# Two weight pairs instead of four beside attention, with conversion spread over more steps

## The chip, the cores and the metric

The kernel runs on one core of a Trainium2 chip. A core has TensorE (PE in the profile, with its weight loads as PEld), VectorE (DVE), ScalarE (ACT), GpSimd (POOL) and SyncE (SP, which here only issues DMAs). The metric is the time of one execution on the device in microseconds; less is better.

## The reference

Three layers follow one another on 2304 tokens of 512 features.

```python
# 1. block-causal attention: 4 batches, 8 heads, 576 tokens, 64 features a head
scores = q @ k.T / 8;  mask: key block (64 tokens) not later than the query's block
attn = softmax(scores);  x = attn @ v          # x: [2304, 512]
# 2. squared ReLU, d_ff = 2048
h = x @ w_in;  g = s * relu(h)**2 + b;  x = g @ w_out
# 3. top-1 of 8 experts, each [512, 1024] and [1024, 512]
e = argmax(x @ w_gate + bias[modality]);  out = gate[e] * (relu(x @ w1[e]) @ w2[e])
```

`moe_w_in` and `moe_w_out` reach the kernel as float64, and float32 precision is kept by splitting each operand into a high and a low part, so that each product is three matmuls (`PASSES`: high-high, high-low, low-high).

## The kernel before

**Attention** (`attention`, lines 25 to 254) is a generator. It works on 16 units, each two heads of one batch (a batch has four units), and each unit has nine steps, one for each block of 64 queries: 144 steps, and some more in which the last ones drain. Step t issues the scores of its block (matmuls L137 and L140, the row maximum L142 on DVE, the exponential L147 on ACT), the normalising of the step before (reciprocal L159 on DVE, product L160 on POOL), the transposes of the block of five steps before (L179, copied by L185), and P·V seven steps after the scores (L202, copied by L204). The ninth step of a unit has two row maxima, the others one. When a unit is done, its 128 features of x go to DRAM (`xT_d`, L207), from which the next layer reads them.

**The squared-ReLU layer** (`SquaredRelu`) takes tokens in 9 blocks of 256 and d_ff in 8 pairs of 256 columns. `load_x` reads a block's x (L311), and makes its high part on ACT (L314) and its low part on DVE (L315). `hidden` does one pair on one block: 24 matmuls (L377), ReLU on ACT (L381), square on DVE (L382), high and low part of the result (L385, L386). `project` multiplies by that pair's rows of `w_out`: 6 matmuls for each half of the block (L392).

Blocks 0 to 5 can begin beside attention, since their tokens lie in batches that are done before the last (`begun` is 6). Blocks 6 to 8 hold tokens of the last batch. `NA` says how many pairs each of the first six blocks does beside attention: 2 for block 0 and 4 for the others, 22 pair-blocks in all. `_beside` cuts this work into pieces: for each block one piece for x, one for each pair, and two for the projections, whose sums go to DRAM (`part_d`, L417). `plan` lists the block of each piece, `NA + 3` for each block, 40 pieces. The main loop emits piece n after step `PIECE_0 + n * PIECE_D`, if its weights and its tokens are ready; the pieces that are left come after the loop:

```python
            while (emitted < len(plan) and step >= PIECE_0 + emitted * PIECE_D
                   and converted >= 4 * NA[plan[emitted]] + 3 and done >= ...):
                next(pieces)
                emitted += 1
        for _ in pieces:
            pass
```

**Conversion.** A pair's weights are four chunks. `convert` handles one chunk in three turns: the DMA of 512 KB (L320); the float64 bits made float32 by three instructions on DVE (L329 to L331); the high part on ACT (L364) and then the low part on POOL (L335). `CONV` lists the steps in which a turn is taken: 19 turns for 16 chunks, at steps 8, 12, ... 80. A turn's instructions stand behind the attention instructions issued last on their engines.

**The next stage** (`after`, L419) does what is left, in groups of one block and a range of pairs: first pairs 0 to 4 of the late blocks 6, 7 and 8; then pairs `NA[blk]` to 4 of the begun blocks (before: block 0 alone, pairs 2 and 3); then pairs 4 to 8 of all blocks in the order 6, 7, 8, 0, ... 5. Beside this the other four pairs are converted (`load_w`, all on DVE and ACT), one chunk for each unit (a unit here is one pair on one block). A group's x is loaded during the group before it; there are two buffers for it. Sums of earlier pairs are read back from `part_d` (L601), added to the new ones (`collect`, L609, or copied where there are none, L611), and written again or, at the end, passed to the router. The layers after this are untouched by the change.

The order of each engine's instructions is fixed before the run by a planner, which takes them by the order of emission and lets later ones go ahead only where they are ready by its own estimate.

Of the kernel before, what the change touches and what calls it, by code (L numbers as in the profile page):

```python
# [278 lines left out]
class SquaredRelu:  # L279
# [115 lines left out]
    def beside(self, ctx, blocks):  # L395

        self.pools(ctx, "a", 1, 2, max(NA), "raw cv xr x r g")
        rows = ctx.enter_context(self.tc.tile_pool(name="ma_rows", bufs=1))
        return self._beside(blocks, rows)

    def _beside(self, blocks, rows):
        nc, D = self.nc, self.D
        for blk in blocks:
            x = self.load_x(blk)
            yield blk
            g = []
            n = NA[blk]
            for p in range(n):
# [11 lines left out]
    def after(self, ctx, rt, begun, free, routed):  # L420

        nc = self.nc
        wz = ctx.enter_context(self.tc.tile_pool(name="m_wz", bufs=1, reuse_waits="tile"))
        self.pools(ctx, "b", 2, 2, 3, "r g xr raw cv x")
        wb = ctx.enter_context(self.tc.tile_pool(name="m_wb", bufs=1, reuse_waits="tile"))
        self.banks(ctx, "b", 4)
        late = list(range(begun, self.NB))
        order = late + list(range(begun))  # L430
        half = max(NA)
        groups = [(blk, 0, half) for blk in late] + [(blk, NA[blk], half) for blk in range(begun) if NA[blk] < half]
        groups += [(blk, half, self.NP) for blk in order]
        units = [(n, p) for n, (_, p0, p1) in enumerate(groups) for p in range(p0, p1)]
        later = (None for p in range(half, self.NP)
                 for _ in self.load_w(wz if p == self.NP - 1 else wb, p, WB_ENG(nc)))
        x, rows, px, g = {}, {}, {}, {}
        x[0] = self.load_x(groups[0][0])
        last, steps = None, iter(())
        for n in range(len(units) + 1):  # L440
            if n < len(units):
                at, p = units[n]
                blk, p0, p1 = groups[at]
                with self.tc.issue_after(self.low_last.ins) if n else nullcontext():
                    next(later, None)
                while p not in self.wo:
                    next(later)
                g[n] = self.hidden(x[at], p)
                if p == p1 - 1:
                    del x[at]  # L450
                if p == max(p1 - 3, p0) and at + 1 < len(groups):
                    x[at + 1] = self.load_x(groups[at + 1][0])
            if last is not None:
                steps = rt.block(*last)
                if last[0] == order[-2]:
                    for _ in steps:
                        pass
                    routed()
                last = None
            next(steps, None)  # L460
            if n == 0:
                continue
            at, p = units[n - 1]
            blk, p0, p1 = groups[at]
            if p == p0:
                rows = rt.rows(blk, self.part_d if p0 else None)
                px = [self.ps_x.tile([P, self.D], F32, name=f"px{t}", tag=f"x{t}") for t in range(2)]
            for t in range(2):
                self.project(px[t], g[n - 1], p, t, p == p0, p == p1 - 1)
            del g[n - 1]  # L470
            if p == p1 - 1:
                rt.collect(px, rows, p0)
                if p1 > half:
                    last = (blk, rows)
                else:
                    for t, r in enumerate(rows):
                        nc.sync.dma_start(self.part_d[blk * TB + t * P:blk * TB + (t + 1) * P], r[:, 0:self.D])
                if at + 1 < len(groups) and groups[at + 1][2] > half >= p1:
                    free()
        return last  # L480
# [5 lines left out]
SMALL = 4  # L486
S_WAIT = 3
TB = 256
NA = (2, 4, 4, 4, 4, 4)
MORE = 0  # L490
NH_A = 1
BANKS_A = (3, 2, 1)
WB_ENG = lambda nc: nc.vector
CONV = [8 + 4 * n for n in range(19)]
PIECE_0 = 50
PIECE_D = 2.8
WA_ENG = lambda nc: nc.gpsimd
PASSES = ((0, 0), (0, 1), (1, 0))

# [1 line left out]
class Router:  # L501
# [7 lines left out]
    def __init__(self, nc, persist, ident, modality_id, w_gate, modality_bias, x2_d):  # L509
# [7 lines left out]
        t = lambda n, sh, dt=F32: persist.tile(sh, dt, name=n)  # L517
        self.NA = self.NI + TINY + SMALL
        self.gidx = t("gidx", [P, self.NA], I32)
        self.sidx = t("sidx", [P, self.NA], I32)  # L520
# [633 lines left out]
@with_exitstack  # L1154
def kernel(
    ctx: ExitStack,
    tc: tile.TileContext,
    q: bass.AP,
    k: bass.AP,
    v: bass.AP,  # L1160
    moe_w_in: bass.AP,
    moe_w_out: bass.AP,
    moe_s: bass.AP,
    moe_b: bass.AP,
    moe2_modality_id: bass.AP,
    moe2_w_gate: bass.AP,
    moe2_modality_bias: bass.AP,
    moe2_w1: bass.AP,
    moe2_w2: bass.AP,
    out: bass.AP,  # L1170
):
    nc = tc.nc
    NT, D = out.shape
    const = ctx.enter_context(tc.tile_pool(name="const", bufs=1))
    dram = ctx.enter_context(tc.tile_pool(name="dram", bufs=1, space=bass.MemoryType.DRAM))
    ident = const.tile([P, P], F32, name="ident")
    make_identity(nc, ident)
    xT_d = dram.tile([D, NT], F32, name="xT_d")
    x2_d = dram.tile([NT, D + 1], F32, name="x2_d")
    rt = Router(nc, const, ident, moe2_modality_id, moe2_w_gate, moe2_modality_bias, x2_d)  # L1180
    part_d = dram.tile([NT, D], F32, name="part_d")
    ex = Experts(nc, tc, ident, rt, x2_d, moe2_w1, moe2_w2, out)
    ffn = SquaredRelu(nc, tc, const, xT_d, moe_w_in, moe_w_out, moe_s, moe_b, part_d)
    c1 = ctx.enter_context(ExitStack())
    w_a = c1.enter_context(tc.tile_pool(name="m_wa", bufs=1, side="right"))
    B, H, S, _ = q.shape
    per = H // 2 * S // 64
    begun = (B - 1) * S // TB + MORE
    with ExitStack() as c2, ExitStack() as early:
        pieces = ffn.beside(c2, range(begun))  # L1190
        banks = Banks()
        banks.open(early, tc, 0, *BANKS_0)
        plan = [blk for blk in range(begun) for _ in range(NA[blk] + 3)]
        emitted = converted = 0
        conv = ffn.convert(w_a, range(max(NA)), WA_ENG(nc))
        for step, done in enumerate(attention(nc, tc, c2, banks, ident, q, k, v, xT_d)):
            if step == per:
                early.close()
                banks.open(c2, tc, 1, *BANKS_A)
                ffn.banks(c2, "a", NH_A)  # L1200
            for _ in range(CONV.count(step)):
                with ExitStack() as behind:
                    for i in banks.last.values():
                        behind.enter_context(tc.issue_after(i.ins))
                    converted += next(conv, 0)
            while (emitted < len(plan) and step >= PIECE_0 + emitted * PIECE_D
                   and converted >= 4 * NA[plan[emitted]] + 3 and done >= H // 2 * (1 + (plan[emitted] * TB + TB - 1) // S)):
# [5 lines that stand above are left out]
    def free():  # L1213
        c1.close()
        ex.open_raw(c1)

    def routed():
        rt.early()
        ex.load_early(0)

    ps_g = ctx.enter_context(tc.tile_pool(name="r_ps_g", bufs=2, space=PSUM, reuse_waits="tile"))
    rt.open(ctx, tc, ps_g, NT - begun * TB)
    with ExitStack() as c3:
        last = ffn.after(c3, rt, begun, free, routed)
    ex.open(ctx)
    ex.xs = {i: ex.gather(i, NT - TB) for i in range(EARLY)}
    with tc.issue_after(ex.gathered.ins):
        ex.load_early(1)
    with tc.high_priority():
        for _ in rt.block(*last):  # L1230
            pass
        rt.finish(ctx, tc)
    ex.run()
# [32 lines left out]
```

## Time and profile before

| | us |
|---|---|
| median of 3 runs (lowest, highest) | 933.21 (931.95, 936.05) |
| the profiled execution | 934.42 |
| its span, first to last instruction | 932.8 |
| PE busy in the span | 899.4 (96%) |
| DVE busy | 590.8 (63%) |
| ACT busy | 520.3 (56%) |
| POOL busy | 214.4 (23%) |

The span has three parts. Attention with the pieces beside it takes until about 352 us, where the first group of the next stage begins. That stage lasts until about 650 us, and the experts until about 921 us. Times in the rows count from the start of the span. A busy PE has a matmul in its pipeline; a matmul's record is longer than the distance to the next one. The table is of the whole span and says nothing about a single stage, so the rows below are taken by stretch.

### The profile page before, as it was taken

The page shows a single profiled execution, that of the slowest core. Times are in us where ns is not written, and L with a number is a line of the kernel's source. Part 1 is how long each engine was busy: PE and PEld are TensorE (multiplying, and loading weights), DVE is VectorE, ACT ScalarE, POOL GpSimd, SP SyncE. Part 2 cuts the span into 40 slices and gives each one's busy share as a digit, 9 for nine tenths or more (in the row PEclk, how much of TensorE's full clock was granted, in tenths as well). Part 3 has the DMA queues.
Part 4 walks back from the last instruction along what each step waited for, and adds up shares of the span by engine and source line. Part 5 has one row for each costly group of instructions (what it writes and reads, how often), then busy time and mean ns, then how long its engine had stood idle before and what let it go on. Part 6 is the DMA issues. An engine that isn't in the chain of part 4 may idle for free. (4 is left out here: it accounts for less than half of the span.)

```text
span 932.8 us, 16292 instructions
## 1 busy us (share of the span) xinstructions
PE 899.4 (96%) x5529; PEld 721.6 (77%) x5529; DVE 590.8 (63%) x1368; ACT 520.3 (56%) x1105; POOL 214.4 (23%) x319
## 2 busy tenths in 40 slices
PE   7989999999999999999999999999999999999995
PEld 5666777787878888889988888888467776766774
DVE  5888876373546445778444454446688887786762
ACT  6878786575757543333232233222288786776763
POOL 4576656132322200000000000002024322221110
PEclk9999999999999999999999999999999999999998
DMA  6565563221231133446022111114246796538400
GB/s 145 137 171 134 160 169 77 73 65 58 69 87 43 37 107 110 138 145 208 30 68 68 59 58 67 46 46 166 106 143 225 245 376 238 200 124 280 153 24 26
DMA packets 109477, 113.79 MB, mean 122 GB/s; under 512 B 62679, under 2 KB 80617, under 8 KB 109387
## 3 DMA queue, kind: packets, MB, share of 16 engines
q1 hardware_dynamic: 105579, 100.74, 34.7%
q0 software_dynamic: 3808, 11.94, 3.6%
q8 instruction: 46, 0.75, 0.4%
q14 instruction: 44, 0.36, 0.1%
HBM read 143.58 MB, written 19.80 MB: 175 GB/s over the span
## 5 line engine op out<-in xcount | busy, mean ns | idle before, releaser
L377 PE MATMUL ph<-xh,wih 128*128 128x256 f32 x576 | 162.9, 283 | 0.0
L377 PE MATMUL ph<-xh,wil 128*128 128x256 f32 x576 | 162.5, 282 | 0.0
L377 PE MATMUL ph<-xl,wih 128*128 128x256 f32 x576 | 162.2, 282 | 0.0
L160 POOL TENSOR_TENSOR p<-p,rc 128x64 f32<-128x64 f32 (+2 forms) x144 | 110.3, 773 | 138.9 <-DVE rc L159 71.4
L381 ACT ACTIVATE r<-ph 128x512 f32<-128x512 f32 x72 | 43.0, 597 | 163.3 <-PE ph L377 138.2
L382 DVE SCALAR_TENSOR_TENSOR r<-r,sc 128x512 f32<-128x512 f32 x72 | 55.8, 775 | 93.5 <-ACT r L381 92.9
L377 PEld LDWEIGHTS ph<-xh,wih 128*128 128x128 f32 x576 | 109.1, 189 | 3.6 <-ACT r L381 0.9
L377 PEld LDWEIGHTS ph<-xl,wih 128*128 128x128 f32 x576 | 109.2, 190 | 2.3
L377 PEld LDWEIGHTS ph<-xh,wil 128*128 128x128 f32 x576 | 109.3, 190 | 0.1
L142 DVE TENSOR_REDUCE nm<-sc 128x1 f32<-128x288 f32 (+8 forms) x160 | 70.8, 450 | 53.9 <-PE sc L140 43.6
L147 ACT ACTIVATE p<-sc,nm 128x288 f32<-128x288 f32 (+8 forms) x160 | 80.5, 506 | 24.2 <-DVE nm L142 10.8
L902 DVE TENSOR_TENSOR w1l<-raw,w1h 128x1024 fp32r<-128x1024 f32 x60 | 71.7, 1223 | 24.6 <-ACT w1h L901 23.2
L392 PE MATMUL px<-woh,gh 128*128 128x512 f32 x200 | 81.6, 408 | 0.0
L392 PE MATMUL px<-woh,gl 128*128 128x512 f32 x200 | 78.6, 394 | 0.0
L392 PE MATMUL px<-wol,gh 128*128 128x512 f32 x200 | 78.5, 393 | 0.0
L902 DVE TENSOR_TENSOR w2l<-raw,w2h 128x1024 fp32r<-128x1024 f32 x64 | 74.7, 1217 | 6.0 <-ACT w2h L901 5.9
L910 POOL DMA_INDIRECT xr<-x_d,gidx_e x2 | 2.3, 1133 | 317.6 <-DMA raw<-in_moe_w_dram 317.3
L901 ACT CAST w2h<-raw 128x1024 fp32r<-128x1024 f32 x64 | 66.3, 1051 | 11.6 <-PE py L993 11.5
L179 PE MATMUL tp<-ident,p 128*128 128x128 f32 x400 | 65.9, 280 | 5.5 <-POOL p L160 3.9
L385 ACT ACTIVATE gh<-r,sc 128x512 fp32r<-128x512 f32 x72 | 52.2, 724 | 34.0 <-DVE r L382 34.0
L901 ACT CAST w1h<-raw 128x1024 fp32r<-128x1024 f32 x60 | 61.6, 1051 | 10.1 <-PE ph L978 8.8
L185 ACT COPY pt<-tp 128x512 f32<-128x512 f32 (+3 forms) x128 | 61.7, 497 | 8.7 <-PE tp L179 8.1
(279 smaller groups left out, 1972.9 us busy)
## 6 DMA issues: line engine op xcount, KB each, us to landing
raw<-in_moe_w_dram SPq DMA_DIRECT2D x172, 512.0 KB
xr<-xT_d SPq DMA_DIRECT2D x19, 512.0 KB
wr<-in_moe_w_in_dram SPq DMA_DIRECT2D x16, 512.0 KB
wr<-in_moe_w_out_dram SPq DMA_DIRECT2D x16, 512.0 KB
row<-part_d SPq DMA_DIRECT2D x20, 256.0 KB
x_d<-row SPq DMA_DIRECT2D x18, 256.5 KB
xT_d<-x SPq DMA_DIRECT2D x16, 288.0 KB
raw_q<-in_q_dram SPq DMA_DIRECT2D x32, 128.0 KB
```

Of the source, the lines that this page charges most:

```text
L142: ps.last["max"] = nc.vector.tensor_reduce(nm[:, e:e + 1], sc[:, 0:w], AX.X, ALU.max, negate=True)
L147: ps.last["exp"] = nc.scalar.activation(pr[:, k0:k0 + w], scs[e][:, 0:w], AF.Exp, bias=nm[:, 0:1], accum_out=sm[:, e:e + 1])
L160: ps.last["scale"] = nc.gpsimd.tensor_mul(pr[:, 0:n], pr[:, 0:n], rc.to_broadcast([P, n]))
L179: nc.tensor.transpose(t[:, e * P:(e + 1) * P], st[u][i][0][:, c * P:(c + 1) * P], ident)
L185: P_COPY(nc, i0)(o, src)
L377: nc.tensor.matmul(ph[:, e], self.wi[p][w][:, c, e * P:(e + 1) * P], x[a][:, c], start=(n == 0), stop=(n == 3 * KC - 1))
L381: nc.scalar.activation(r, ph, AF.Relu)
L382: nc.vector.scalar_tensor_tensor(r, r, self.sc[:, 0:1], r, ALU.mult, ALU.mult)
L385: nc.scalar.activation(gh, r, AF.Identity, bias=self.sc[:, 1:2])
L392: self.nc.tensor.matmul(px, g[a][:, e, t * P:(t + 1) * P], self.wo[p][w][:, e], start=(first and e == 0 and n == 0), stop=(last and e == 1 ...
L901: self.nc.scalar.copy(ws[0][c], r)
L902: self.nc.vector.tensor_sub(ws[1][c], r, ws[0][c].bitcast(F32))
```

## The change

Every begun block does two pairs beside attention: 12 pair-blocks in 30 pieces. Pairs 2 and 3 are still converted beside attention (`HALF` keeps the number of pairs, 4, that `max(NA)` gave before), and all six begun blocks do them in the next stage, in six groups of two pairs instead of one. The turns of conversion are taken at steps 8, 14, ... 68 (eleven turns, after which the first eight chunks are ready) and 74, 82, ... 130. Pieces are due from step 70 in distances of 2.45 steps.

```diff
-        half = max(NA)
+        half = HALF
         groups = [(blk, 0, half) for blk in late] + [(blk, NA[blk], half) for blk in range(begun) if NA[blk] < half]
...
-NA = (2, 4, 4, 4, 4, 4)
+NA = (2, 2, 2, 2, 2, 2)
+HALF = 4
...
-CONV = [8 + 4 * n for n in range(19)]
-PIECE_0 = 50
-PIECE_D = 2.8
+CONV = [8 + 6 * n for n in range(11)] + [74 + 8 * n for n in range(8)]
+PIECE_0 = 70
+PIECE_D = 2.45
...
-        conv = ffn.convert(w_a, range(max(NA)), WA_ENG(nc))
+        conv = ffn.convert(w_a, range(HALF), WA_ENG(nc))
```

The number of buffers for the results of `hidden` beside attention is `max(NA)`, and so falls from 4 to 2.

## Rows read from the trace of the kernel before

**Rows 1.** Stretches: length, busy time (instructions) by engine, granted clock, DMA share, GB/s.

```profile
20.10:80.20 60.10, 52.77 (x361) 39.44 (x362) 51.37 (x165) 50.02 (x164) 37.79 (x63) 0.97 0.56 145
80.20:150.80 70.60, 65.75 (x459) 50.56 (x460) 58.36 (x172) 56.77 (x176) 44.98 (x67) 1.00 0.58 157
150.80:326.30 175.50, 174.25 (x1176) 143.21 (x1175) 89.96 (x280) 107.43 (x306) 53.79 (x108) 1.00 0.23 62
326.30:357.00 30.70, 30.30 (x203) 25.28 (x202) 12.90 (x26) 13.18 (x27) 2.19 (x2) 1.00 0.37 122
357.00:650.00 293.00, 292.90 (x1949) 262.43 (x1948) 165.01 (x409) 90.47 (x150) 2.34 (x3) 1.00 0.28 88
418.50:430.30 11.80, 11.80 (x76) 10.58 (x75) 10.02 (x16) 4.64 (x9) 0.00 (x0) 1.00 0.72 207
```

**Rows 2.** Stretches, instructions of line 142 alone (row maxima, DVE).

```profile
20.10:80.20 60.10, 17.81 (x40) 0.97 0.56 145
80.20:150.80 70.60, 17.55 (x40) 1.00 0.58 157
189.50:305.10 115.60, 22.17 (x51) 1.00 0.22 61
```

**Rows 3.** Stretches, instructions of line 381 alone (one for each hidden group, ACT).

```profile
326.30:357.00 30.70, 2.40 (x4) 1.00 0.37 122
352.00:419.00 67.00, 7.14 (x12) 1.00 0.39 124
419.00:431.00 12.00, 1.19 (x2) 1.00 0.74 210
361.60:463.00 101.40, 10.71 (x18) 1.00 0.41 130
```

**Rows 4.** Stretches, line 377 alone (hidden: PE, PEld).

```profile
80.20:150.80 70.60, 10.26 (x72) 9.13 (x72) 1.00 0.58 157
189.50:305.10 115.60, 33.38 (x257) 31.25 (x256) 1.00 0.22 61
```

**Rows 5.** Stretches, line 392 alone (projection: PE, PEld).

```profile
80.20:150.80 70.60, 6.16 (x24) 4.35 (x24) 1.00 0.58 157
189.50:305.10 115.60, 23.36 (x96) 17.69 (x96) 1.00 0.22 61
```

**Rows 6.** Waits, 20.1 to 80.2 us: total us, times, longest.

```profile
PE tp L179 <- POOL p L160: 3.1, 4, 1.9
POOL p L160 <- DVE rc L159: 10.5, 11, 2.6
```

**Rows 7.** Groups of instructions, 20.1 to 80.2 us: busy us, mean ns, idle before.

```profile
L330 DVE SCALAR_TENSOR_TENSOR f<-wr,f 128x512 int32<-128x512 int32 x8 | 7.8, 970 | 0.0
L331 DVE SCALAR_TENSOR_TENSOR f<-wr,f 128x512 int32<-128x512 int32 x8 | 6.2, 769 | 0.0
L329 DVE TENSOR_SCALAR f<-wr 128x512 int32<-128x512 int32 x8 | 5.7, 716 | 1.9 <-DMA wr<-in_moe_w_in_dram 0.9 <-DMA wr<-in_moe_w_out_dram 0.7 <-POOL wol L335 0.3
```

**Rows 8.** Timeline around the end of attention: start us, us, instruction.

```profile
325.98 0.30 PE L140 MATMUL sc<-kh,ql 128*128 128x288 f32 x1
...
328.87 1.15 POOL L160 TENSOR_TENSOR p<-p,rc 128x576 f32<-128x576 f32 x1 [0.51 <-ACT x L204]
...
335.17 2.42 PE L202 MATMUL o<-pt,raw_v 128*64 128x320 f32 x20
...
340.54 8.02 SPq L311 DMA_DIRECT2D xr<-xT_d  x2
...
345.85 1.05 ACT L314 CAST xh<-xr 128x1024 fp32r<-128x1024 f32 x1 [0.69 <-DMA xr<-xT_d]
...
346.93 1.22 DVE L315 TENSOR_TENSOR xl<-xr,xh 128x1024 fp32r<-128x1024 f32 x1 [0.98 <-ACT xh L314]
```

**Rows 9.** Stretches around the one fall of the clock, columns as in rows 1.

```profile
49.40:51.80 2.40, 0.57 (x4) 0.42 (x4) 2.38 (x10) 0.52 (x3) 1.33 (x2) 1.00 0.43 98
51.80:55.20 3.40, 3.36 (x15) 3.18 (x15) 3.14 (x10) 3.35 (x13) 1.94 (x3) 0.50 1.02 258
```

## The prediction

> **What bounds the kernel now.** I read the stretches first, to see which engine is full in which stage. From 150.8 us on TensorE (PE) is full: 174.25 of 175.50 us, 30.30 of 30.70 and 292.90 of 293.00, with VectorE (DVE) and ScalarE (ACT) far below. Before that it is not: 52.77 of 60.10 and 65.75 of 70.60 us, and there DVE (51.37, 58.36) and ACT (50.02, 56.77) are nearly as full [rows 1]. So work that only changes its place costs nothing from 150.8 us on, and whatever PE loses or regains in the first 150 us, or in a new hole, goes into the end one to one.
>
> The second reading is the pitch of attention. The score reductions count steps: ten are one unit of nine steps. 20.10 to 80.20 us holds 40 of them, 36 steps (9 to 44); 80.20 to 150.80 the next 36 (45 to 80); 189.50 to 305.10 holds 50 and one of the next unit, 45 steps [rows 2]. One weight pair on one block (a pair-block: 24 matmuls into `ph`, 12 into `px`) takes 101.40 / 18 = 5.63 us where PE does nothing else [rows 3]. In the 45 full steps PE also did 256 / 24 = 10.7 hidden halves and 96 / 12 = 8 projection halves of pair-blocks [rows 4, 5], 9.33 pair-blocks or 52.6 us; the other 63.0 us are 1.40 us a step. That is attention's price on a full PE. At it the first 36 steps cost 50.4 us and took 60.1: 9.7 lost. The next 36 cost 50.4 and, with 72 and 24 matmuls of feed-forward [rows 4, 5], 2.5 pair-blocks or 14.1 us; they took 70.6: 6.1 lost. So 15.8 us stand there to be regained (12.2 by PE's busy time alone, [rows 1]).
>
> The third reading is why. PE's longest wait there is for POOL's normalised scores (3.1 us), and POOL's is for a reciprocal on DVE: 10.5 us in 11 waits [rows 6]. DVE is held by conversion: 716 + 970 + 769 ns are 2.46 us a chunk, eight of them in these 36 steps [rows 7], 19.6 of the 60.1 us.
>
> The fourth reading is the hand-over to the next stage, below.
>
> **The change, part by part.**
>
> *Ten pair-blocks move* from beside attention to the next stage (22 to 12 beside it, 50 to 60 after). PE's cost is the same in both places: 10 x 5.63 = 56.3 us go and come back, sum 0. On ACT and DVE each takes its two instructions with it. Bounds: nothing below, since the matmuls are the same; above, whatever the next stage cannot hide.
>
> *Five more groups* of two pairs there: five more loads of x (512 KB), casts (1.05 us on ACT) and differences (1.22 on DVE [rows 8]), ten part reads, ten part writes, ten sums from PSUM. The profile holds one such group already, that of block 0: DVE 10.02 of 11.80 us with conversion still running, PE 11.80 [rows 1]. So 0. Of the six such groups only the first two meet conversion, since its 16 chunks go one to a unit and the first twelve units belong to the late blocks. If the cover goes (an SP queue where a part write, waiting for its sum, stands ahead of the next x load), the next x is late; at 2 us a group 10 us.
>
> *Conversion spread out.* Between steps 9 and 44 six chunks are converted instead of eight or nine, and from step 70 one in eight steps. All 16 chunks stay beside attention; their loads, casts and POOL differences go with them, in the same order on each queue. Of DVE's 51.37 us this takes some 2.5 x 2.46 = 6. Waiting should fall faster than load, so I halve the loss per step: 9.7 becomes 4.9 for steps 9 to 44. Steps 45 to 69 now run without feed-forward work at the same density of chunks: 25 x 0.135 = 3.4. Steps 70 to 80, with both again, 0.3. Together 8.6 lost instead of 15.8: **7.2 us gained**. Bounds: all 15.8 gained; or, if ACT (50.02 of 60.10) sets the pace and not conversion, 9.7 + 25 x 0.27 + 0.5 = 16.9 lost, so 1.1 worse. I take the half because DVE and ACT are about equally full.
>
> The Trainium skill (Perfetto Trace Analysis, Identifying the Most-Contended Engine) says matmul busy time does not show a PE's reserve and that weight-load busy time does. By it the two stretches (39.44 of 60.10 and 50.56 of 70.60 us, against 143.21 of 175.50 in the full stretch [rows 1]) hold 11.8 + 8.6 = 20.4 us, and halved in the same way the sum below would come out 2 us lower; it speaks against my forecast, not enough to turn its sign.
>
> *Steps 81 to 143* lose 1.25 + 0.40 us now [rows 1]. With 2 pair-blocks in 12.25 steps instead of 4 in 19.6 there is a fifth less to fill waits with. I add **1.0 us** (0 to 3). The results of `hidden` there have two buffers instead of four, so a block's first pair waits for the last projection of the block before. That one is emitted two pieces earlier, 4.9 steps or 6.9 us at 1.40; I cost this at 0 (at most some 1 us for each of five blocks).
>
> *Where the pieces end.* This is the part that decides. The first late block, 6, holds tokens of the last batch, so its x cannot be read before attention's last unit is written. Now 40 pieces are due at steps 50 + 2.8 n: those of block 5 come at steps 143 to 160, past the last scores (step 143). Four hidden groups of block 5 come after 326.3 us [rows 3]. After the change the last of 30 pieces is due at 70 + 29 x 2.45 = 141.05: the leftover is gone. PE's order follows the order of emission in the trace (last scores, transposes, block 5's hidden groups, last P·V).
>
> What the leftover covers: attention's last P·V ends at 335.17 + 2.42 = 337.59 us; its copy, the write of xT, the read of x (issued 340.54, cast begins 345.85), the cast and the difference end at 346.93 + 1.22 = 348.15 [rows 8]. That is 10.6 us in which PE has nothing else: block 7's x, the only other one with a buffer, has the same cause. The blocks that are ready do not slip forward: after 352 us the groups run in program order, twelve units of the late blocks and then two of block 0 [rows 3]. Ahead of it, attention's drain: last scores end at 326.28, POOL's last product at 330.02 [rows 8]; without two hidden groups between, transposes, copies and P·V of 2.42 us follow directly, and PE waits for perhaps 2.0 us of it (estimate, 1 to 3). Together **12.6 us**. Bounds: 9.0 (10.6 + 1.0, less half of the read's 5.3 us if fewer transfers run beside it), and 13.6.
>
> After such a hole the clock falls. In this trace PE was busy 0.57 of 2.40 us, and was then granted 0.50 (1.2 instead of 2.4 GHz) for 3.40 us [rows 9]: **1.7 us** of work lost (0 to 3.4).
>
> **Sum.** 12.6 + 1.7 + 1.0 - 7.2 = +8.1 us. The profiled execution took 934.42 us (span 932.8 and 1.6 around it), 1.2 above the median of 933.21. 934.4 + 8.1 = 942.5, or 941.3 against the median: **941 us**, 0.9% slower.
>
> **Rivals.**
>
> B, *the hole is filled*: the planner lays block 5's last pieces, whose inputs come late, behind attention's drain. Only gain and thinning remain: 933.2 + 1.0 - 7.2 = 927. For it: the planner goes by its own estimate and not by the emission alone. Against it: what it lets slip is later work brought forward, not earlier work held back. This is the side of faster; it decides if at least 8 us of feed-forward work stand behind the last scores.
>
> C, *conversion was the whole loss*: PE is full from step 9 on and the hole stays. 12.6 + 1.7 + 1.0 - 15.8 = -0.5: 933, no change. For it: the chain PE, POOL, DVE of [rows 6]. Against it: ACT at 83%.
>
> D, *conversion was none of it*: ACT sets the pace, steps 45 to 69 run bare. 12.6 + 1.7 + 1.0 + 1.1 = 16.4: 950. For it: ACT's share hardly falls with four chunks less. Against it: the waits end at DVE.
>
> E, *the next stage stalls on its short groups*: at 2 us for five more groups, 8.1 + 10 = 18: 951. Against it: block 0's group, 11.80 of 11.80.
>
> **How the numbers follow.** My forecast 0.48 (its own range 935 to 946), B 0.18, C 0.16, D 0.12, E 0.06. A difference under 0.5% (4.7 us) cannot be told from none here. Slower: 0.42 of my own, D, and half of E: 0.57. Same: the rest of my own, most of C, part of E: 0.22. Faster: B and the edge of C: 0.21. The range 929 to 949 leaves out the deeper part of B and the ends of D and E.
>
> **What would show it.** Right: between the last P·V and the first matmul of the next stage PE idles some 10 us, followed by a stretch at 0.50; steps 9 to 44 take about 55 us; from there to the routing PE is full; that stage is 56 us longer. Wrong: PE busy through the hand-over (B); a pitch of 1.4 (C) or above 1.6 us (D) in steps 9 to 69; waits of `ph` for x in the two-pair groups (E).

## The result, and the profile after

The changed kernel takes 938.70 us (median of 13 runs, 937.37 to 941.40), the kernel before 933.46 in the same session (13 runs). The ratio is 1.0057, 95% interval 1.0048 to 1.0066: slower by about 5.3 us, just past what can be told from no change. The forecast was 941. The profiled executions stand a little closer together, 937.96 against 934.42, spans 936.0 against 932.8; the sums by stage below are for this pair, so they have to explain 3.2 us.

First the stretches of the changed kernel, cut at the same steps as [rows 1]: steps 9 to 44, 45 to 80, 81 to the start of the last row maximum, the hand-over in two parts, and the next stage. Columns as in [rows 1].

```profile
20.10:76.30 56.20, 51.39 (x370) 38.66 (x369) 45.00 (x161) 49.08 (x164) 33.47 (x61) 1.00 0.60 157
76.30:141.10 64.80, 60.88 (x428) 47.15 (x428) 52.68 (x166) 54.47 (x172) 40.31 (x64) 1.00 0.56 146
141.10:283.80 142.70, 141.16 (x981) 115.08 (x980) 89.44 (x283) 103.11 (x302) 60.57 (x114) 1.00 0.31 89
283.80:300.20 16.40, 6.36 (x52) 4.00 (x50) 5.72 (x15) 6.22 (x15) 1.21 (x1) 0.81 0.50 162
300.20:304.40 4.20, 4.16 (x18) 3.87 (x19) 1.21 (x1) 0.00 (x0) 0.00 (x0) 0.51 0.43 122
304.40:655.00 350.60, 350.51 (x2310) 313.87 (x2310) 194.25 (x446) 109.30 (x176) 4.33 (x5) 1.00 0.31 99
```

The first two rows took 60.1 and 70.6 us before and take 56.2 and 64.8 now, and DVE's share of the first has fallen from 85 to 80%. The fourth row is new: PE is busy in 6.36 of 16.40 us, and in the fifth it runs at 0.51. From 304.4 us on it is full again, in a stage that is now longer.

The hand-over by the timeline; the waits of PE between 270 and 310 us (total, times, longest) stand behind it.

```profile
283.84 0.30 PE L140 MATMUL sc<-kh,ql 128*128 128x288 f32 x1
...
286.78 1.21 POOL L160 TENSOR_TENSOR p<-p,rc 128x576 f32<-128x576 f32 x1 [3.10 <-DVE id L563]
...
289.37 2.42 PE L202 MATMUL o<-pt,raw_v 128*64 128x320 f32 x20 [0.56 <-ACT pt L185]
...
294.58 0.37 SPq L311 DMA_DIRECT2D xr<-xT_d  x1
...
299.10 1.04 ACT L314 CAST xh<-xr 128x1024 fp32r<-128x1024 f32 x1 [6.32 <-DMA xr<-xT_d]
300.18 1.23 DVE L315 TENSOR_TENSOR xl<-xr,xh 128x1024 fp32r<-128x1024 f32 x1 [6.62 <-ACT xh L314]
300.20 1.22 PE L377 MATMUL ph<-xh,wih 128*128 128x256 f32 x4 [8.41 <-ACT xh L314]
```

```profile
PE ph L377 <- ACT xh L314: 8.4, 1, 8.4
PE tp L179 <- POOL p L160: 0.9, 1, 0.9
PE o L202 <- ACT pt L185: 0.6, 1, 0.6
PE tp L179 <- ACT pt L185: 0.2, 1, 0.2
```

These are the lines that answer to [rows 8]: the same chain from the last scores over P·V, the write and the read of x to the cast, but nothing runs on PE beside it. It idles 0.2 + 0.9 + 0.6 in attention's drain and 8.4 us behind the last P·V, 10.1 in all. The clock around it (columns as in [rows 9]):

```profile
289.50:294.10 4.60, 2.29 (x20) 1.12 (x20) 1.44 (x3) 0.94 (x2) 0.00 (x0) 1.00 0.21 69
294.10:300.20 6.10, 0.00 (x1) 0.00 (x1) 0.02 (x1) 1.04 (x1) 0.00 (x0) 0.50 0.77 255
300.20:304.30 4.10, 4.06 (x17) 3.77 (x18) 1.21 (x1) 0.00 (x0) 0.00 (x0) 0.50 0.43 123
```

The granted clock fell to 0.50 (1.2 of 2.4 GHz) after 2.29 busy us of 4.60, and PE's first 4.1 us of work after the hole were done at that rate, 2.05 us lost. The matmuls show it: 0.41 us each there and 0.28 later.

```profile
302.05 0.41 PE L377 MATMUL ph<-xh,wih 128*128 128x256 f32 x1
...
304.51 0.28 PE L377 MATMUL ph<-xh,wih 128*128 128x256 f32 x1
```

**The loss by stage.** With the prices of the prediction (1.40 us a step, 5.63 a pair-block) every stretch has a loss: its length less its steps and its pair-blocks. The first two stretches have 36 steps each, the third 62, since it ends where the last step's row maximum begins. The counts behind the changed kernel's are 48 and 24 matmuls (2 pair-blocks) in the second stretch and 240 and 120 (10) in the third; L377 and then L392:

```profile
76.30:141.10 64.80, 8.45 (x48) 6.79 (x48) 1.00 0.56 146
141.10:283.80 142.70, 31.53 (x240) 29.53 (x240) 1.00 0.31 89
```

```profile
76.30:141.10 64.80, 6.52 (x24) 4.22 (x24) 1.00 0.56 146
141.10:283.80 142.70, 30.84 (x120) 21.68 (x120) 1.00 0.31 89
```

The fourth column goes from the last score's row maximum to the first transpose of an expert's hidden layer (655.2 us before, 658.3 after), less the remaining pair-blocks; it holds some 25 us of other work, the same in every kernel. So only differences mean something. All kernels below are in the table. The last two columns come from each kernel's own runs, with the ratio to the kernel before on the same chip; the sums come from one profiled execution each.

| kernel | 9 to 44 | 45 to 80 | 81 to 143 | from the last scores | sum | median us | ratio (95%) |
|---|---|---|---|---|---|---|---|
| before | 9.7 | 6.1 | 1.0 | 25.2 | 42.0 | 933.5 to 934.1 | |
| after | 5.8 | 3.1 | -0.4 | 36.7 | 45.2 | 938.70 | 1.0057 (1.0048, 1.0066) |
| e1 begun blocks first | 6.2 | 3.1 | 0.8 | 30.0 | 40.1 | 932.32 | 0.9980 (0.9967, 0.9992) |
| e2 later pieces | 5.0 | 4.0 | 1.2 | 30.0 | 40.2 | 934.77 | 1.0012 (1.0002, 1.0022) |
| e3 before, bare hand-over | 8.6 | 4.6 | 2.0 | 36.7 | 51.9 | 945.05 | 1.0123 (1.0107, 1.0139) |
| e4 old conversion | 10.9 | 10.0 | 0.6 | 39.1 | 60.6 | 951.03 | 1.0171 (1.0146, 1.0195) |
| e5 four pairs on block 5 | 6.2 | 4.0 | 1.9 | 25.7 | 37.8 | 930.04 | 0.9961 (0.9949, 0.9973) |
| e6 useless work in the hole | 6.2 | 3.1 | 0.3 | 38.7 | 48.3 | 938.73 | 1.0057 (1.0035, 1.0080) |
| e7 old conversion, early pieces | 9.7 | 7.9 | 1.3 | 38.8 | 57.7 | 948.97 | 1.0160 (1.0146, 1.0174) |
| e8 low part on DVE | 8.6 | 3.6 | -2.0 | 37.1 | 47.3 | 939.37 | 1.0061 (1.0048, 1.0075) |
| e9 spread alone | 6.2 | 4.7 | 0.6 | 24.8 | 36.3 | 929.41 | 0.9952 (0.9939, 0.9964) |
| e10 thinner spread | 6.7 | 4.7 | 1.7 | 25.3 | 38.4 | 931.18 | 0.9969 (0.9957, 0.9982) |

For the change: -3.9 and -3.0 from the conversion's stretches, -1.4, and +11.5 at the hand-over: +3.2, the difference of the spans. Three of the sums (e2, e4, e6) belong to a profiled execution 2 to 3 us away from its median, and that of e7 to one 1.8 us away, so for them the runs count and not the sum.

How far a column repeats can be read off as well. Six kernels have the same conversion up to step 68 and no pieces before step 70 (after, e1, e2, e5, e6, e9): their first column goes from 5.0 to 6.2. In the four with the conversion of the kernel before (before, e3, e4, e7) it goes from 8.6 to 10.9. After, e1 and e6 share all of attention: their third column goes from -0.4 to 0.8. So a difference of about 1 us in one column says nothing by itself.

**Where the clock fell.** In steps 9 to 44 each of the four kernels with conversion as before has a stretch at 0.50: 3.4 us from 51.8 in the kernel before [rows 9], from 49.2 in e3 and from 51.0 in e7, 6.8 us from 49.5 in e4. None of the seven with spread conversion and the low part on POOL (after, e1, e2, e5, e6, e9, e10) has one there. PE was busy in 3.36 of the 3.40 us [rows 9], so up to 1.7 of the 3.9 us that the change wins in these steps is half clock that no longer occurs, not shorter waits.

### The profile page after: what moved, and what is told of

It is laid out like the page before. It is cut to its first block, busy times and chain, and to the rows that moved or that the text cites. A ratio compares the mean times of both kernels' runs of the same rounds, so it can differ in the third digit from the quotient of the medians.

```text
span 936.0 us, 16360 instructions
## 1 busy us (share of the span) xinstructions
PE 896.0 (96%) x5529; PEld 721.6 (77%) x5529; DVE 600.4 (64%) x1383; ACT 524.0 (56%) x1110; POOL 210.6 (22%) x319
## 5 line engine op out<-in xcount | busy, mean ns | idle before, releaser
L377 PE MATMUL ph<-xh,wih 128*128 128x256 f32 x576 | 163.0, 284 | 8.4 <-ACT xh L314 8.4
L377 PE MATMUL ph<-xl,wih 128*128 128x256 f32 x576 | 163.1, 283 | 0.0
L377 PE MATMUL ph<-xh,wil 128*128 128x256 f32 x576 | 162.9, 283 | 0.0
L160 POOL TENSOR_TENSOR p<-p,rc 128x64 f32<-128x64 f32 (+2 forms) x144 | 107.4, 757 | 120.6 <-DVE rc L159 63.2
L377 PEld LDWEIGHTS ph<-xh,wih 128*128 128x128 f32 x576 | 109.9, 191 | 11.2 <-ACT xh L314 8.5
L377 PEld LDWEIGHTS ph<-xl,wih 128*128 128x128 f32 x576 | 109.8, 191 | 3.0 <-DVE xl L315 0.3
L377 PEld LDWEIGHTS ph<-xh,wil 128*128 128x128 f32 x576 | 109.9, 191 | 0.1
L392 PE MATMUL px<-woh,gh 128*128 128x512 f32 x240 | 97.4, 406 | 0.0
L392 PE MATMUL px<-woh,gl 128*128 128x512 f32 x240 | 94.6, 394 | 0.0
L392 PE MATMUL px<-wol,gh 128*128 128x512 f32 x240 | 94.2, 393 | 0.0
L903 DVE TENSOR_TENSOR w1l<-raw,w1h 128x1024 fp32r<-128x1024 f32 x60 | 71.7, 1224 | 24.7 <-ACT w1h L902 21.9
```

Source lines behind the costliest of these rows:

```text
L160: ps.last["scale"] = nc.gpsimd.tensor_mul(pr[:, 0:n], pr[:, 0:n], rc.to_broadcast([P, n]))
L377: nc.tensor.matmul(ph[:, e], self.wi[p][w][:, c, e * P:(e + 1) * P], x[a][:, c], start=(n == 0), stop=(n == 3 * KC - 1))
L392: self.nc.tensor.matmul(px, g[a][:, e, t * P:(t + 1) * P], self.wo[p][w][:, e], start=(first and e == 0 and n == 0), stop=(last and e == 1 ...
L903: self.nc.vector.tensor_sub(ws[1][c], r, ws[0][c].bitcast(F32))
```

## The experiments

The theory was the prediction's: two effects against one another, the spread that wins ahead of step 81 and the bare hand-over that costs more.

### e1: begun blocks first

```diff
-        groups = [(blk, 0, half) for blk in late] + [(blk, NA[blk], half) for blk in range(begun) if NA[blk] < half]
+        groups = [(blk, NA[blk], half) for blk in range(begun) if NA[blk] < half] + [(blk, 0, half) for blk in late]
```

> The changed kernel, but the six two-pair groups of the begun blocks come first in the next stage and the late blocks 6 to 8 after them. Theory (the hole at the hand-over is what costs, and it is there because the first group's x needs attention's last unit): block 0's x is in DRAM long before, so PE goes on after the last P.V; the 8.4 us hole and the half-clock stretch behind it (2.1 us) go: about 928 us, 5 under the kernel before. Rival (the next stage cannot start earlier in any case, since its x buffers lie where attention's tiles lay): the read and casts still start after attention, a hole of some 6 us stays, 935 to 937. Rival (the loss sits in the short groups of the next stage): no change, 938 to 939.

932.32 us, 6.4 less than the changed kernel and a little less than the kernel before. It lies between the theory's 928 and the rival's 935 to 937. Most of the hole is gone, not all. The four longest of PE's waits between 286 and 300 us:

```profile
PE ph L377 <- ACT xh L314: 1.5, 1, 1.5
PE tp L179 <- POOL p L160: 0.9, 1, 0.9
PE ph L377 <- DVE xl L315: 0.8, 1, 0.8
PE o L202 <- ACT pt L185: 0.6, 1, 0.6
```

8.4 us have become 1.5 + 0.8: block 0's x was read early (issued at 265.2 us), but its cast began 0.4 us after the last P·V ended and not before, and the drain's waits are as they were. So the theory holds for the cause (the first group's x), the rival for the rest: the cast waits for attention's end. Whether it is for the memory, or only because it stands on ACT behind the copy of the last P·V, was not tried. And against the theory the clock still fell, after 2.37 busy us of 4.60:

```profile
293.00:297.60 4.60, 2.37 (x22) 1.75 (x19) 2.41 (x4) 1.37 (x2) 0.00 (x0) 1.00 0.54 167
297.60:301.00 3.40, 3.40 (x19) 3.40 (x18) 1.23 (x2) 0.86 (x2) 0.00 (x0) 0.50 0.90 249
```

11.5 became 4.8 us.

### e2: later pieces

```diff
-PIECE_D = 2.45
+PIECE_D = 2.9
```

> The changed kernel with pieces due in distances of 2.9 steps instead of 2.45, so that block 5's two hidden groups and its projections come behind the last scores (2 pair-blocks, 11.3 us). Theory: they fill the hole, PE idles under 1 us there and the clock does not fall: about 928 us. Rival (steps 45 to 143 are too thin, and PE loses there): they become thinner by a sixth, 938 or more.

934.77 us: 3.9 won, where the theory said 11. PE's waits between 270 and 300 us:

```profile
PE ph L377 <- ACT xh L314: 2.3, 1, 2.3
PE ph L377 <- DVE xl L315: 0.5, 1, 0.5
PE pxa L392 <- ACT rowa L416: 0.5, 1, 0.5
```

The drain is covered now (none of its waits is left), but of the 11.3 us of leftover work half stood in front of the last P·V and only the projections behind it, 5.6 us against a chain of 8.4. And the clock fell to 0.50 for 3.4 us all the same:

```profile
294.00:297.20 3.20, 1.52 (x10) 1.32 (x11) 1.23 (x1) 1.04 (x1) 0.00 (x0) 1.00 0.63 230
297.20:300.60 3.40, 3.40 (x18) 3.40 (x17) 0.00 (x0) 0.00 (x0) 0.00 (x0) 0.51 0.56 159
```

What the expectation missed is where in the hand-over the leftover stands. The rival's 938 or more did not come. Steps 45 to 80 and 81 to 143 lost 4.0 and 1.2 against 3.1 and -0.4; whether thinner steps cost about 1 us the columns cannot tell.

### e3: the kernel before with a bare hand-over

```diff
-PIECE_D = 2.8
+PIECE_D = 2.3
```

> The kernel before with pieces due in distances of 2.3 steps instead of 2.8: all 40 come ahead of the last scores, nothing is left for the hand-over. Theory: the same hole of 8 to 10 us opens in a kernel whose conversion and pairs are unchanged, and the clock falls behind it: 943 to 945 us. Rival (the hole is not what decides; the changed kernel is slower by its moved pairs): about 933, as before.

945.05 us, 11.0 over the kernel before and a little over the forecast's upper end. Conversion, pairs and groups are those of before; the hand-over is that of the changed kernel, in the stretches from the last scores to the first matmul of the next stage and behind it:

```profile
346.00:362.30 16.30, 6.34 (x51) 3.98 (x49) 5.93 (x17) 6.70 (x17) 2.25 (x2) 0.82 0.49 155
362.30:366.60 4.30, 4.25 (x18) 3.96 (x19) 1.22 (x1) 0.00 (x0) 0.00 (x0) 0.50 0.38 114
```

16.30 us with 6.34 busy, then 4.30 at 0.50, against 16.40 with 6.36 and 4.20 in the changed kernel. So the price of the bare hand-over, 11.0 us in the runs and 11.5 in the fourth column, is measured by itself. It is the same with 22 pair-blocks beside attention as with 12.

### e4: conversion as before

```diff
-CONV = [8 + 6 * n for n in range(11)] + [74 + 8 * n for n in range(8)]
+CONV = [8 + 4 * n for n in range(19)]
```

> The changed kernel with conversion as before, one turn in four steps from 8 to 80. Theory (spreading it won some 7 us in steps 9 to 80 and hides part of the hole's price): most of that is lost again, 942 to 945 us, steps 9 to 44 take 60 us instead of 56. Rival (ScalarE sets the pace of attention, conversion does not matter; the 4 us won there have another cause): 938 to 940, and 56 us.

951.03 us: 12.3 more than the changed kernel, well above the theory's 3 to 6. Its first two stretches, same steps:

```profile
19.60:80.80 61.20, 53.56 (x361) 40.41 (x362) 51.10 (x165) 49.99 (x164) 37.38 (x63) 0.94 0.56 143
80.80:152.50 71.70, 66.66 (x454) 49.86 (x453) 59.15 (x182) 57.66 (x178) 50.79 (x80) 1.00 0.62 165
```

Steps 9 to 44 take 61.2 us as forecast, 5.1 more than with the spread. But steps 45 to 80 take 71.7 with the same 2 pair-blocks as the changed kernel's 64.8: 6.9 more. Ahead of its last 10 us the profiled execution was granted half the clock in four stretches (from 49.5, 155.3, 302.1 and 308.9 us), the changed kernel's in one. PE was busy for 12.4 us more at half clock than there, so up to 6.2 us of what e4 lost is the clock. The rival, by which conversion does not matter, falls: ACT did 49.99 us of work in steps 9 to 44, 0.9 more than in the changed kernel, and the steps took 5.1 longer.

### e5: four pairs on block 5

```diff
-NA = (2, 2, 2, 2, 2, 2)
+NA = (2, 2, 2, 2, 2, 4)
...
-PIECE_D = 2.45
+PIECE_D = 2.85
```

> The changed kernel, but block 5 does four pairs beside attention as before and its pieces are due past the last scores (distance 2.85 steps), so the hand-over has the same four hidden groups and two projections of four pairs (22.5 us) as the kernel before. Theory (the change is two things that pull against one another: spread conversion wins 7 to 8 us ahead of step 81, the bare hand-over costs 11.5): with the hand-over closed only the gain is left, 926 to 928 us, and the loss of the stretch from the last scores on is again that of the kernel before. Rival (closing it only moves the wait, as 11.3 us of leftover work won 4 us and not 11): 932 or more.

930.04 us, 8.7 less than the changed kernel and 0.39% less than the kernel before. Two microseconds short of the forecast, but the hand-over is what it was before (25.7 against 25.2), and from 3 us behind the last scores on 40 us are full at the full clock:

```profile
279.90:320.00 40.10, 39.77 (x263) 34.10 (x262) 19.30 (x32) 15.30 (x27) 1.15 (x1) 1.00 0.30 97
```

What was left of the 7 to 8 us is 3.5 + 2.1 - 0.9 - 0.5 = 4.2 by the stages. The rival (closing it only moves the wait) falls.

### e6: work of no use in the hole

```diff
+        with tc.issue_after(banks.pv.ins):
+            idle = ffn.ps_x.tile([P, 512], F32, name="pxd", tag="x")
+            for n in range(32):
+                nc.tensor.matmul(idle, ffn.wi[0][0][:, n % 4, 0:P], ffn.wo[0][0][:, n % 2], start=True, stop=True)
```

(`banks.pv` is the last P·V matmul.)

> The changed kernel with 32 matmuls of no use (into a PSUM tile that nothing reads) right behind attention's last P.V, 7.5 us of TensorE work inside the 8.4 us hole; all other work is as it was. Theory (behind the hole TensorE runs at half clock for 4.2 us of work, which costs 2.1 us of the 11.5): the clock stays up and the time falls by about 2 us, to 936.5. Rival (the whole price is the idle time): 938.7, or some tenths more where the useless work ends late.

938.73 us in the median, no difference, but with runs from 936.7 to 943.3. In the profiled execution (941.50 us) the clock fell earlier, in attention's drain:

```profile
288.40:291.10 2.70, 1.23 (x10) 0.81 (x11) 2.60 (x5) 1.40 (x4) 0.92 (x1) 1.00 0.04 13
291.10:294.50 3.40, 3.40 (x18) 1.42 (x16) 0.51 (x1) 0.00 (x0) 0.00 (x0) 0.50 0.00 0
...
304.80:308.20 3.40, 3.40 (x18) 3.40 (x18) 0.00 (x0) 0.00 (x0) 0.00 (x0) 0.50 0.54 154
```

The last P·V ran at half clock (4.06 us instead of 2.42), which made x later, and the clock fell once more after the wait that was left. The other runs suggest that this is not always so. Each run's mean granted clock is on record: the profiled one has 0.993, and e5, e9 and e10, whose traces show no stretch at 0.50 ahead of their last 10 us, have 0.995 to 0.997. Of the six runs of e6 three have 0.996 or 0.997, and took 936.73, 936.84 and 937.85 us; those at 0.993 took 939.61 and 941.50, and the one at 0.989 took 943.27. So where the clock seems to have stayed up, the theory's 936.5 came, 1.9 us under the changed kernel, whose runs have 0.988 to 0.992; the median of all six hides it. That is a split made after the fact, with three runs on its side, but it agrees with the 2.05 us read from the trace.

### e7: conversion as before, pieces from step 50

```diff
-CONV = [8 + 6 * n for n in range(11)] + [74 + 8 * n for n in range(8)]
-PIECE_0 = 70
-PIECE_D = 2.45
+CONV = [8 + 4 * n for n in range(19)]
+PIECE_0 = 50
+PIECE_D = 3.15
```

> The changed kernel with conversion as before (one turn in four steps) and pieces from step 50 in distances of 3.15, so that feed-forward work stands in steps 50 to 70 again; the hand-over stays bare. To be read against the same kernel with pieces from step 70 (951.0). Theory (work beside attention fills TensorE's waits, so bare steps 45 to 70 cost while conversion presses): steps 45 to 80 lose 6 us as in the kernel before and not 10, about 946. Rival (conversion alone sets the pace of these steps, whatever runs beside): 951, with 10 us lost.

948.97 us, 2.1 under e4 where 5 were expected. Steps 45 to 80 lose 7.9 us, between the theory's 6 and the rival's 10. The runs of the two kernels overlap (947.8 to 950.8 here, 946.6 to 953.7 for e4), so it is not shown that feed-forward work beside attention fills PE's waits there. What is shown is that most of what old conversion costs stays.

### e8: the low part on DVE

```diff
-WA_ENG = lambda nc: nc.gpsimd
+WA_ENG = lambda nc: nc.vector
```

> The changed kernel with the low part of each converted chunk on VectorE (0.7 us) instead of GpSimd (1.4 us). Theory (a chunk's block of VectorE instructions, which the reciprocals and row maxima have to wait for, is what holds attention): 16 x 0.7 = 11 us more on VectorE ahead of step 130, some 3 to 5 us slower, 942 to 944. Rival (GpSimd, whose products of normalised scores wait behind the 1.4 us subtractions, holds it): 3 us or more faster, 936 or less. If neither, 938 to 940.

939.37 us, +0.7: neither. Steps 9 to 44, which have no feed-forward work, lose 8.6 instead of 5.8, which looks like the theory, but a finer cut speaks against it. The first low part comes at step 26, so the stretches to compare are steps 27 to 44 and steps 45 to 69, which run nearly bare too. First the changed kernel, then e8:

```profile
47.39:76.29 28.90, 25.23 (x183) 18.99 (x183) 22.83 (x80) 24.88 (x83) 18.49 (x32) 1.00 0.56 143
76.29:116.66 40.37, 37.13 (x266) 27.86 (x265) 33.63 (x109) 34.79 (x113) 27.36 (x43) 1.00 0.51 130
```

```profile
47.25:78.99 31.74, 27.15 (x181) 20.12 (x180) 23.72 (x83) 24.81 (x82) 14.16 (x29) 0.95 0.49 128
78.99:119.06 40.07, 37.10 (x267) 28.07 (x266) 35.60 (x113) 35.91 (x115) 20.41 (x38) 1.00 0.53 141
```

All of the difference is in steps 27 to 44, and up to 1.7 us of it is a stretch at 0.50 (3.4 us from 68.5 us), ahead of which PE's longest waits were for ACT (1.8 and 1.5 us). In steps 45 to 69, where four low parts moved against three, e8 is 0.3 us shorter. So no run shows that DVE's instructions for a chunk are what PE waits for. The rival, that GpSimd holds attention, falls: 936 or less did not come.

### e9: spread alone

```diff
-NA = (2, 2, 2, 2, 2, 2)
+NA = (2, 4, 4, 4, 4, 4)
...
-CONV = [8 + 6 * n for n in range(11)] + [74 + 8 * n for n in range(8)]
+CONV = [8 + 6 * n for n in range(11)] + [71 + 3 * n for n in range(8)]
...
-PIECE_D = 2.45
+PIECE_D = 2.2
```

> All 22 pair-blocks stay beside attention as in the kernel before; only conversion is spread (the first eleven turns at 8, 14, ... 68, the other eight in distances of 3 to 92) and the pieces moved behind it (from step 70 in distances of 2.2, so that all of block 5 comes past the last scores). Theory (the place of a pair-block costs nothing once TensorE is full; the spread wins, the hand-over decides): as the kernel with four pairs on block 5 alone, 929 to 931. Rival (fewer pair-blocks beside attention were needed for the gain): 933 or more. A third: the eight late turns in three-step distances cost again what the first win, 933 to 935, seen as a loss in steps 70 to 92.

929.41 us, the fastest of all, 0.48% under the kernel before, and not distinguishable from e5. All 22 pair-blocks are beside attention; the hand-over is full:

```profile
320.70:361.60 40.90, 40.90 (x281) 35.50 (x280) 20.10 (x37) 17.12 (x33) 2.19 (x2) 1.00 0.37 116
```

So the gain needed no pair to move. The late turns in three-step distances cost 1.6 us in steps 45 to 80 against the changed kernel (4.7 to 3.1), less than the third case had it. The buffers for the results of `hidden` are four again here, as in e5 and e10; their number was not tried by itself.

### e10: thinner spread

```diff
-NA = (2, 2, 2, 2, 2, 2)
+NA = (2, 2, 2, 2, 2, 4)
...
-CONV = [8 + 6 * n for n in range(11)] + [74 + 8 * n for n in range(8)]
-PIECE_0 = 70
+CONV = [8 + 7 * n for n in range(19)]
+PIECE_0 = 80
```

> The kernel with four pairs on block 5 (930.0), with conversion one turn in seven steps from 8 to 134 and pieces from step 80 in distances of 2.85. Theory (the loss ahead of step 81 goes with the density of conversion): steps 9 to 44 lose 5 us instead of 6.2; ten more bare steps cost about 1: 929 to 930. Rival (bare steps cost as much as thinner conversion wins, or more): 930.5 to 933.

(The pieces' distance stayed 2.45, so that block 5 comes past the last scores from step 80; the expectation's 2.85 is a slip.) 931.18 us, in the rival's range, no better than e5. Steps 9 to 44 lose 6.7, not 5: below one turn in six steps thinner conversion wins nothing here. That the later start of the pieces costs something is not shown: the ratios of e5 and e10 overlap.

## Why the prediction was right

The sign and the mechanism held: 941 forecast, 938.7 measured, with the hole, the half clock behind it and the shorter steps ahead of step 81 where it said. The size held less well: +8.1 us forecast, +5.3 measured. The sum is right in sign because the hand-over costs more than the spread wins; both are measured apart, in e3 and in e9.

- **Ten pair-blocks move: 0.** Held. PE is full in the longer stage, and e9 against e5 points the same way for the opposite move: 8 pair-blocks more beside attention, with other late turns of conversion, 0.6 us apart.
- **Five more short groups: 0.** Held. The changed kernel's stretch over them has PE at 56.00 of 56.00 us; rival E (a stall in the short groups) falls.

```profile
376.00:432.00 56.00, 56.00 (x360) 50.49 (x359) 32.18 (x44) 19.12 (x28) 0.00 (x0) 1.00 0.48 158
```

- **Conversion spread: 7.2 gained.** 6.9 in the profile, in the parts forecast: 5.8 lost in steps 9 to 44 (4.9 forecast) and 3.1 in steps 45 to 80 (3.7). That it is conversion is shown by e4. That it is DVE's part of conversion, the third reading, is not shown: e8 put more on DVE and lost no more in steps 45 to 69. Halving the loss was a choice between two bounds that no row fixed, and that it came out this near is in part luck; up to 1.7 us of it is half clock, which the prediction did not tell apart in this term. One thing the sum hid: 7.2 was a net of the spread and of the bare steps 45 to 69. Under these late pieces the spread is worth 12.3 us in the runs (e4), its part of the clock included.
- **Steps 81 to 143: +1.0.** Too dear: -1.4 in this profile, -0.2 and -0.7 in e1 and e6 with the same attention. The thinner filling there cost nothing that shows, and neither did the two buffers, which the prediction put at 0; PE stayed full (141.16 of 142.70).
- **The bare hand-over: 12.6.** The mechanism held (e1, e3, e5). The term was too large: 10.1 us idle. The read took 4.5 us and not 5.3. And the chain ends earlier than I put it: four hidden groups have a PSUM tile each, so PE starts with the first high-high matmul of four of them when the cast is done and does not wait for the low part, 1.2 us less.
- **The clock: 1.7.** 2.05 by the trace, about 1.9 by the runs of e6 in which it seems to have stayed up.
- **Sum.** +8.1 forecast, +3.2 in the profiled pair and +5.3 in the runs. In the profiled pair the hand-over with its clock was 2.8 us too dear (14.3 forecast, 11.5 measured; 0.4 of it is what PE idled there in the kernel before, too), steps 81 to 143 were 2.4 too dear, and the gain was 0.3 too large: 8.1 - 2.8 - 2.4 + 0.3 = 3.2. The 2 us between the profiled pair and the runs are not placed in a stage.

Rival B (a filled hole) falls by the waits of the changed kernel. C (conversion as the whole loss) falls too: 8.9 of 15.8 us stay in steps 9 to 80, and thinner conversion in e10 wins nothing more. What holds these 8.9 us is open: e8 does not show that it is DVE, and ACT is busy in 87% of steps 9 to 44 (49.08 of 56.20), but no run took work from it. D (no gain) falls by e4.

## What to carry to other kernels

When one stage's leftover runs beside the next stage's start, it is the cover of the hand-over: see what the first instruction of the next stage waits for, add up that chain, and keep as much independent work behind the last instruction that feeds it, not merely behind the last scores. A change that both thins a pressed stretch and moves the cover's end should be cut in two; here the one half alone is worth -0.5% (e9) and the other +1.2% (e3).

## What was not expected of the hardware

Here the clock fell without a long hole. In e6 it fell to 0.50 after 2.70 us in which PE was busy 1.23 us, with no wait above 0.9 us; in the kernel before it fell after 0.57 busy us of 2.40, with no wait above 1.9 us [rows 6, rows 9]. In the same place it seems to fall in some runs and not in others: the runs of e6 spread over 6.5 us, those with a mean granted clock of 0.996 or more at the low end. The same can be seen in e1, whose runs go from 929.62 us at 0.996 to 934.24 at 0.992. The traces of e5, e9 and e10, whose hand-over is full or nearly so, have no stretch at 0.50 before their last 10 us, and their runs lie within 1.4, 2.9 and 2.8 us.
